# Attention with position bias, two expert layers: score products on 64 rows, the last half tile per head, cheaper relus, weight differences also on GpSimd

## The chip, the cores and the metric

One core of one Trainium2 chip. The metric is the device time of one execution in microseconds, the median of three runs. Five engines work side by side: TensorE (PE, matrix products, with its weight loads PEld), VectorE (DVE), ScalarE (ACT), GpSimd (POOL), and SyncE (SP), which issues the transfers.

## What is computed

Attention over 2 batches, 8 heads, 576 positions, 64 numbers a head, with a bias that a small network makes of the distance of two positions; then a layer of four experts with a gate; then a gated layer.

```python
scores = scale * np.matmul(q, k.transpose(0, 1, 3, 2))
psi_rel = np.log1p(np.abs(rel))
psi_i = np.log1p(np.maximum(pos[:, None].astype(np.float32), 1.0))
x = (psi_rel / psi_i)[..., None]
h = np.maximum(x @ w1 + b1, 0.0)
bias = h @ w2
scores = scores + bias.transpose(2, 0, 1)[None, :, :, :]
scores = scores - np.max(scores, axis=-1, keepdims=True)
attn = np.exp(scores)
attn = attn / (np.sum(attn, axis=-1, keepdims=True) + 1e-09)
return np.matmul(attn, v).astype(np.float32)
...
for e in range(E):
    h = np.maximum(x @ w1[e], 0.0)
    out += p[:, e:e + 1] * (h @ w2[e])
...
return (a * b @ w_out).astype(np.float32)
```

## The kernel before, in words

Everything is written as a list of operations with the engines that may take each, an estimate of its time, a rank and the buffers that it needs; `Plan.run` (L139) walks through the list in estimated time and writes out, engine by engine, the order in which instructions are issued. On the chip each engine follows its own order and waits for semaphores. An operation with `lock` isn't placed on DVE and POOL at the same time as another such.

*Exact products.* PE works on rounded numbers (`fp32r`); to keep precision an operand is split into a rounded part (cast on ACT or DVE) and the rest (a subtraction): `wh`, `wl` for weights (`unit`, L629: cast `whi`, subtraction `wlo`), `qh`, `ql` for queries, `x_hi`, `x_lo` for the layer's input. A product then takes three rounded ones (hi x hi, lo x hi, hi x lo).

*Bias.* `bias_group` (L348) makes 16 rows of the bias at a time, 36 groups: four relus over the table of logarithms, each `max(table * w1 / psi, -b1)` with two operands per partition, three of them on DVE (L357) and one on ACT (L359); four products `pb` on 32-column pieces of the array (L371); `side` and `mirror` write the two arms of the rows (L389, L391; the mirror on POOL is a copy, L396); a transfer stores them in DRAM (`bias_d`, L406). A score tile reads its bias from there (`bt`, L463; three transfers for the last half tile, L465 to L468).

*Attention.* Four pairs of heads `m`, two batches `b`, tiles `t` of 128 queries: t = 0 first for all eight (m, b), then (1, 2) and (3, 4); tile 4 has 64 queries. `step` (L474) takes two heads `s`: scores `ps`, for t = 0 on plain float32 keys and 64-row products, the two key halves on the two row halves of the array (L513); for the others 128-row products (L495): keys lie in 128 partitions, rounded part in the upper 64 and rest in the lower 64, queries are stored twice, so that `qh` and `ql` times these keys are two products for each key half. Then DVE adds the bias and takes the minimum (L498), ACT takes the exponential (L508), PE transposes (`pt`, L524, L541), ACT or DVE copies to `ptb`. Tile 4 puts both heads in one tile of 128 partitions, each with 64 rows. `values` (L554) takes the reciprocals of the sums (L564, L565), spreads them (`rx`, `rp`, `rb`), and makes the products with the values on two column halves (`pv`, L589), and `x_hi`, `x_lo`.

*Fill.* The first expert layer's first pass (`up`, L722; `pz`, L733) needs only tile 0 of all heads. It has rank 2, so it fills what attention leaves of PE; its second pass needs all of attention. The gated layer stands behind.

*Buffers.* Four pairs of weight buffers `w` at first, two of queries `q`, two of values `v`, two raw keys `k2` of 2 x 576.

Of the kernel before, what the change touches and what calls it, by code (L numbers as in the profile page):

```python
# [18 lines left out]
HID = 32  # L19
P = 128  # L20
# [22 lines left out]
           "whi": "ACT DVE", "wlo": "DVE", "xhi": "DVE", "xlo": "POOL DVE", "rb": "ACT DVE", "rx": "ACT DVE", "s64": "POOL DVE",  # L43
# [185 lines left out]
def tile_kernel(ctx, tc, qd, kd, kf, vd, cst, probs, w1r, w2r, war, wbr, wor, out):  # L229
# [57 lines left out]
    place(R["q"], ap_, "q", 2, [P, 2, QW], F32R, pair=True)  # L287
    place(R["k2"], ap_, "k2", 2, [P, 2, S])
    place(R["k"], ap_, "k", 3, [P, 2, S], F32R)
# [11 lines left out]
    place(R["w"], mid, "wm", 2, [P, 1024], F32R, pair=True)  # L301
# [14 lines left out]
    cs_t = hp.tile([P, S + S // 4 + 2 + 32], F32, name="cs")  # L316
    cs, negb = Buf(t=cs_t), hp.tile([P, 1], F32, name="negb")
    corr = {n: hp.tile([P, 1], F32, name=f"corr{n}") for n in sorted(set(RELUS.values()))}
    tab, sc = cs_t[:, 0:S], cs_t[:, S:S + S // 4]
    cw, w2s = cs_t[:, S + S // 4:S + S // 4 + 2], cs_t[:, S + S // 4 + 2:]  # L320
    op({"SP": 440}, lambda e: nc.sync.dma_start(out=cs_t, in_=cst), w=[cs], size=P * 3016)

    def scales(e):
        nc.vector.tensor_scalar(out=sc, in0=sc, scalar1=cw[:, 0:1], scalar2=None, op0=ALU.mult)
        nc.vector.tensor_scalar(out=negb, in0=cw[:, 1:2], scalar1=-1.0, scalar2=None, op0=ALU.mult)
        nc.vector.tensor_scalar(out=w2s, in0=w2s, scalar1=8.0, scalar2=None, op0=ALU.mult)

    op({"DVE": 700}, scales, rw=[cs])
# [19 lines left out]
    def bias_group(u, rank):  # L348
# [24 lines left out]
        op({"PE": n * 1.67 + 250}, mm, r=[*hs, cs], w=[pb], hold=[bst], prio=pri)  # L373


        def ends():
            t, o = base()
            b = bst.t
            if before >= after:
                side = b[:, 0:before + 1], t[:, o:o + 1 + before][:, ::-1]  # L380
                rest = b[:, before + 1:before + after], t[:, o + 1:o + after], b[:, before - after + 1:before][:, ::-1]
            else:
                side = b[:, before:before + after], t[:, o:o + after]
                rest = b[:, 0:before], t[:, o + 1:o + 1 + before][:, ::-1], b[:, before + 1:2 * before + 1][:, ::-1]
            return side, rest

        def put(e, out, src):
            if e == "ACT":
                nc.scalar.activation(out=out, in_=src, func=AF.Identity, bias=corr[acts])  # L389
            else:  # L390
                nc.vector.tensor_scalar(out=out, in0=src, scalar1=corr[acts], scalar2=None, op0=ALU.add)  # L391

        def mirror(e):
            rest = ends()[1]
            if e == "POOL":
                nc.gpsimd.tensor_copy(rest[0], rest[2])  # L396
            else:
                put(e, *rest[:2])
# [3 lines left out]
        op({e: v for e, v in {"POOL": 2 * m + 150, "ACT": m / 1.2 + 280, "DVE": m / 0.96 + 200}.items() if e in ENGINES["mirror"].split()}, mirror, r=[pb, cr], w=[bst], after=[side], prio=pri)  # L402
# [16 lines left out]
    QK, fins = {}, []  # L419
# [9 lines left out]
    def plain(m):  # L429
        k2, q2 = new("k2"), new("q2")  # L430
        op({"SP": 440}, lambda e: nc.sync.dma_start(out=k2.t.rearrange("p b n -> p (b n)"), in_=kf[m]), w=[k2], size=P * 8 * S)
        for b in range(B):
            op({"SP": 440}, lambda e, b=b: nc.sync.dma_start(out=q2.t[:, b].rearrange("p (s w) -> p s w", s=2), in_=qd[m, b][:, :, :P]), w=[q2], size=P * 8 * P)
        return k2, q2

    def keys(m, b):
        k2, k = new("k2"), new("k")
        op({"SP": 440}, lambda e: nc.sync.dma_start(out=k2.t, in_=kd[m, b]), w=[k2], size=P * 8 * S)
        op(t_copy(2 * S, ENGINES["kcast"]), lambda e: copy(e, k.t, k2.t), r=[k2], w=[k], prio=RANK["prep"], lock=True)
        op(t_two(2 * S, ENGINES["ksub"]), lambda e: engine[e].tensor_tensor(out=k.t[D:P], in0=k2.t[D:P], in1=f(k.t[D:P]), op=ALU.subtract), r=[k2], rw=[k], prio=RANK["prep"], lock=True)  # L440
        return k

    def queries(m, b, lo, w):
# [3 lines left out]
        op(t_copy(2 * w, ENGINES["qcast"]), lambda e: copy(e, z(q.t[0]), z(q2.t)), r=[q2], w=[q], prio=RANK["prep"], lock=True)  # L447
# [5 lines left out]
    def bias_tile(m, t):  # L453
# [677 lines left out]
```

## Time and profile before

| | |
|---|---|
| median of 3 runs | 836.31 us (834.63 to 836.48) |
| the profiled execution | 831.73 us, span 830.0 us |
| mean granted clock of PE | 0.997 |
| PE busy | 800.1 us (96%) |
| PE's weight loads | 670.2 us (81%) |
| DVE busy | 615.2 us (74%) |
| ACT busy | 342.7 us (41%) |
| POOL busy | 50.6 us (6%) |
| chain that ended last | PE 83%, DVE 10%, DMA 3%, ACT 3% |

A busy PE is not a PE at its peak: records of its products overlap and last longer than the distance from one start to the next. The time between two starts in a stretch without waits tells what a product costs.

### The profile page before, as it was taken

The page shows a single profiled execution, that of the slowest core. Times are in us where ns is not written, and L with a number is a line of the kernel's source. Part 1 is how long each engine was busy: PE and PEld are TensorE (multiplying, and loading weights), DVE is VectorE, ACT ScalarE, POOL GpSimd, SP SyncE. Part 2 cuts the span into 40 slices and gives each one's busy share as a digit, 9 for nine tenths or more (in the row PEclk, how much of TensorE's full clock was granted, in tenths as well). Part 3 has the DMA queues.
Part 4 walks back from the last instruction along what each step waited for, and adds up shares of the span by engine and source line. Part 5 has one row for each costly group of instructions (what it writes and reads, how often), then busy time and mean ns, then how long its engine had stood idle before and what let it go on. Part 6 is the DMA issues. An engine that isn't in the chain of part 4 may idle for free.

```text
span 830.0 us, 12927 instructions
## 1 busy us (share of the span) xinstructions
PE 800.1 (96%) x4939; PEld 670.2 (81%) x4939; DVE 615.2 (74%) x1245; ACT 342.7 (41%) x694; POOL 50.6 (6%) x63
## 2 busy tenths in 40 slices
PE   7878999999999999999999999999999999999998
PEld 3445677888888788888888988888889999899996
DVE  8898886889977768777988898944656565747545
ACT  7885765566667521122122222213345432323211
POOL 1010000101101000000000000000010100100000
PEclk9999999999999999999999999999999999999999
DMA  6988757677564433664566557610302220201103
GB/s 250 341 276 288 226 178 206 198 234 219 186 202 143 136 87 117 190 217 151 141 190 215 165 152 232 201 74 1 102 1 86 68 77 26 77 31 48 51 1 115
DMA packets 48590, 122.38 MB, mean 147 GB/s; under 512 B 5136, under 2 KB 11536, under 8 KB 48528
## 3 DMA queue, kind: packets, MB, share of 16 engines
q1 hardware_dynamic: 48384, 121.42, 45.9%
q8 instruction: 39, 0.64, 0.3%
q14 instruction: 23, 0.19, 0.1%
q10 hardware_dynamic: 144, 0.13, 0.0%
HBM read 95.69 MB, written 25.84 MB: 146 GB/s over the span
## 4 chain that ended last, share of the span: by engine, by line
PE 83%; DVE 10%; DMA 3%; ACT 3%; issue 1%; POOL 0%; DVEq 0%; SPq 0%; ACTq 0%; POOLq 0%
PE pz L733 31%; PE up L722 22%; PE pw L856 9%; PE pr L856 4%; PE pv L589 4%; PE ps L495 3%; PE pt L524 2%; PE pq L856 2%; DVE pr L498 2%; PE pb L371 2%; DMA bt<-bias_d 1%; DVE wl L633 1%; ACT pr L508 1%; DVE hh L357 1%; DVE k L440 1%
## 5 line engine op out<-in xcount | busy, mean ns | idle before, releaser
L733 PE MATMUL pz<-wh,hh 128*128 128x512 f32 x386 | 154.1, 399 | 0.0
L733 PE MATMUL pz<-wl,hh 128*128 128x512 f32 x386 | 152.2, 394 | 0.0
L733 PE MATMUL pz<-wh,hl 128*128 128x512 f32 x386 | 151.7, 393 | 0.2 <-DVE hl L750 0.2
L722 PE MATMUL up<-x_hi,wh 128*128 128x256 f32 (+2 forms) x384 | 132.9, 346 | 1.2 <-DVE hl L750 1.1
L722 PE MATMUL up<-x_hi,wl 128*128 128x256 f32 (+2 forms) x384 | 129.8, 338 | 0.0
L722 PE MATMUL up<-x_lo,wh 128*128 128x256 f32 (+2 forms) x384 | 129.8, 338 | 0.0
L749 ACT ACTIVATE hh<-up 128x256 fp32r<-128x256 f32 (+2 forms) x96 | 47.0, 491 | 149.1 <-PE up L722 148.9
L236 ACT CAST wh<-wst 128x1024 fp32r<-128x1024 f32 (+1 forms) x62 | 62.4, 1006 | 89.4 <-PE pz L733 79.0
L733 PEld LDWEIGHTS pz<-wl,hh 128*128 128x128 f32 x386 | 72.5, 188 | 17.3
L733 PEld LDWEIGHTS pz<-wh,hl 128*128 128x128 f32 x386 | 72.6, 188 | 15.4 <-DVE hl L750 0.7
L733 PEld LDWEIGHTS pz<-wh,hh 128*128 128x128 f32 x386 | 72.5, 188 | 15.4 <-issue 1.2
L633 DVE TENSOR_TENSOR wl<-wst,wh 128x1024 fp32r<-128x1024 f32 x64 | 78.5, 1229 | 8.2 <-ACT wh L236 6.3
L722 PEld LDWEIGHTS up<-x_hi,wh 128*128 128x128 f32 x384 | 72.3, 188 | 13.2 <-issue 2.8
L722 PEld LDWEIGHTS up<-x_lo,wh 128*128 128x128 f32 x384 | 72.4, 188 | 6.4
L722 PEld LDWEIGHTS up<-x_hi,wl 128*128 128x128 f32 x384 | 72.3, 188 | 5.9
L750 DVE SCALAR_TENSOR_TENSOR hl<-up,hh 128x256 fp32r<-128x256 f32 (+2 forms) x96 | 52.8, 553 | 29.4 <-ACT hh L749 29.0
L498 DVE CUSTOM_DVE_ANT_0 pr<-ps,bt 128x576 f32<-128x576 f32 (+1 forms) x80 | 59.6, 751 | 12.9 <-PE ps L495 9.0
L236 ACT COPY ct<-pw 128x512 f32<-128x512 f32 (+3 forms) x48 | 27.8, 580 | 97.8 <-PE pw L856 97.7
L508 ACT ACTIVATE pr<-pr,sums 128x576 f32<-128x576 f32 x72 | 56.0, 777 | 15.1 <-DVE sums L498 14.6
L357 DVE TENSOR_SCALAR hh<-cs,negb 128x576 f32<-128x576 f32 (+17 forms) x108 | 48.4, 504 | 3.8 <-PE pb L371 3.7
L236 ACT COPY ptb<-pt 128x512 f32<-128x512 f32 (+3 forms) x92 | 38.4, 449 | 26.4 <-PE pt L524 24.8
L524 PE MATMUL pt<-ident,pr 128*128 128x128 f32 x288 | 42.8, 277 | 4.2 <-ACT pr L508 3.5
(157 smaller groups left out, 1408.7 us busy)
## 6 DMA issues: line engine op xcount, KB each, us to landing
wst<-in_w1r SPq DMA_DIRECT2D x32, 512.0 KB, 4.3
wst<-in_w2r SPq DMA_DIRECT2D x32, 512.0 KB, 4.3
bias_d<-bst SPq DMA_DIRECT2D x36, 295.5 KB, 3.9
bt<-bias_d SPq DMA_DIRECT2D x16, 576.0 KB, 5.2
v<-in_vd SPq DMA_DIRECT2D x24, 320.0 KB, 4.6
s<-in_war SPq DMA_DIRECT2D x12, 512.0 KB, 5.1
wz_d<-hl SPq DMA_DIRECT2D x24, 256.0 KB, 2.7
s<-in_wbr SPq DMA_DIRECT2D x12, 512.0 KB, 4.9
```

Of the source, the lines that this page charges most:

```text
L236: (nc.scalar.copy if e == "ACT" else engine[e].tensor_copy)(out, in_)
L357: op({"DVE": n / 1.92 + 190}, lambda e, hh=hh, G=G: nc.vector.tensor_scalar(out=hh.t[:, :n], in0=tab[:, :n], scalar1=sc[:, G:G + 1], scala ...
L498: nc.vector.tensor_tensor_reduce(out=pr.t[r0:r1, c].rearrange("p (a b) -> p a b", a=2), in0=ps.t[r0:r1, :, :HS], in1=bt.t[r0:r1, c].rearra ...
L508: nc.scalar.activation(out=pr.t[:, c], in_=pr.t[:, c], func=AF.Exp, scale=-1.0, bias=sums.t[:, neg:neg + 1], accum_out=sums.t[:, col:col + 1])
L524: nc.tensor.transpose(pt.t[:, kt * P:kt * P + P], pr.t[:, s, k0:k0 + P], ident)
L589: nc.tensor.matmul(pv.t[s * D:(s + 1) * D, :w], V.t[:, s, kt * D:(kt + 1) * D], ptb.t[:, blk, :w], start=(kt == 0), stop=(kt == 4))
L633: op(t_two(1024, ENGINES["wlo"]), lambda e: engine[e].tensor_tensor(out=w.t[1], in0=wst.t, in1=f(w.t[0]), op=ALU.subtract), r=[wst], rw=[w ...
L722: nc.tensor.matmul(u.t[:, :n], a[:, d, ft * P:(ft + 1) * P], x[:, d, lo:lo + n], start=(d == 0 and j == 0), stop=(d == 3 and j == 2))
L733: nc.tensor.matmul(z.t, a[:, ft, tt * P:(tt + 1) * P], bb[:, ft, :], start=(first and ft == 0 and j == 0), stop=(final and ft == 1 and j = ...
L749: relu = op({"ACT": n / 1.2 + 68}, lambda en, ft=ft, u=u: nc.scalar.activation(out=h.t[0][:, ft, :n], in_=u.t[:, :n], func=AF.Relu), r=[u] ...
L750: op({"DVE": n / 0.96 + 68}, lambda en, ft=ft, u=u: nc.vector.scalar_tensor_tensor(out=h.t[1][:, ft, :n], in0=u.t[:, :n], scalar=0.0, in1= ...
L856: nc.tensor.matmul(o_, s[:, k], d[:, k], start=(first and k == 0 and i == 0), stop=(k == 1 and i == 2), skip_group_check=True)
```

## The change

Five edits stand in one version.

1. *Scores.* Keys for t > 0 lie as those for t = 0 did: half the keys in the upper 64 partitions and half in the lower. `k` is a pair (`kh`, `kl`) of 128 x 576, split by a cast and a subtraction of 576 columns instead of 1152. A score takes three terms, (qh, kh), (qh, kl), (ql, kh), each as two 64-row products, one for each key half, on the two row halves of the array.
2. *Last half tile.* Tile 4 handles the two heads one after the other with 64 partitions each: two exponentials, nine transposes of 64 rows, one bias transfer instead of three.
3. *Relus.* The table is multiplied by w1 once (on ACT, ahead of the first relu), and the relu is `max(table, -b1 * psi)` with one operand; the division by psi and the correction move into `side`, which multiplies and adds. The mirror is a copy on each engine that may take it.
4. *Weight differences.* `wlo` may go to POOL or DVE, and not to DVE alone.
5. *Buffers.* Raw keys and queries come per (m, b); at the start there is one pair of weight buffers and one of query buffers less, and two raw queries and two values more; when eight of these have been given out, the extra ones return to weights and queries.

```diff
-           "whi": "ACT DVE", "wlo": "DVE", "xhi": "DVE", "xlo": "POOL DVE", "rb": "ACT DVE", "rx": "ACT DVE", "s64": "POOL DVE",
+           "whi": "ACT DVE", "wlo": "POOL DVE", "xhi": "DVE", "xlo": "POOL DVE", "rb": "ACT DVE", "rx": "ACT DVE", "s64": "POOL DVE",
...
+    op({"ACT": S / 1.2 + 200}, lambda e: nc.scalar.activation(out=tab, in_=tab, func=AF.Copy, scale=cw[:, 0:1]), r=[cs], w=[lg], prio=-1)
...
-                op({"DVE": n / 1.92 + 190}, lambda e, hh=hh, G=G: nc.vector.tensor_scalar(out=hh.t[:, :n], in0=tab[:, :n], scalar1=sc[:, G:G + 1], scalar2=negb, op0=ALU.mult, op1=ALU.max), r=[cs], w=[hh], prio=pri, lock=True)
+                op({"DVE": n / 1.92 + 130}, lambda e, hh=hh, G=G: nc.vector.tensor_scalar(out=hh.t[:, :n], in0=tab[:, :n], scalar1=neg_[:, G:G + 1], scalar2=None, op0=ALU.max), r=[cs], w=[hh], prio=pri, lock=True)
...
-                nc.vector.tensor_scalar(out=out, in0=src, scalar1=corr[acts], scalar2=None, op0=ALU.add)
+                nc.vector.tensor_scalar(out=out, in0=src, scalar1=rinv[:, u:u + 1], scalar2=corr[acts], op0=ALU.mult, op1=ALU.add)
...
-        k2, k = new("k2"), new("k")
-        op({"SP": 440}, lambda e: nc.sync.dma_start(out=k2.t, in_=kd[m, b]), w=[k2], size=P * 8 * S)
-        op(t_copy(2 * S, ENGINES["kcast"]), lambda e: copy(e, k.t, k2.t), r=[k2], w=[k], prio=RANK["prep"], lock=True)
-        op(t_two(2 * S, ENGINES["ksub"]), lambda e: engine[e].tensor_tensor(out=k.t[D:P], in0=k2.t[D:P], in1=f(k.t[D:P]), op=ALU.subtract), r=[k2], rw=[k], prio=RANK["prep"], lock=True)
+        k2, k = raw_keys(m, b), new("k")
+        op(t_copy(S, ENGINES["kcast"]), lambda e: copy(e, k.t[0], k2.t), r=[k2], w=[k], prio=RANK["prep"], lock=True, after=guests[-2:])
+        op(t_two(S, ENGINES["ksub"]), lambda e: engine[e].tensor_tensor(out=k.t[1], in0=k2.t, in1=f(k.t[0]), op=ALU.subtract), r=[k2], rw=[k], prio=RANK["prep"], lock=True)
...
-                for kk, qz in enumerate(Q.t):
-                    lhs = qz.rearrange("p s w -> p (s w)")[:, at:at + P]
-                    for n, (half, o, k0, w) in enumerate(runs):
-                        nc.tensor.matmul(ps.t[:, half, o:o + w], lhs, K.t[:, s, k0:k0 + w], start=(kk == 0 and n < 2), stop=(kk == 1 and n in (0, len(runs) - 1)))
+                terms = [(Q.t.rearrange("p s w -> p (s w)"), K.t)] if t == 0 else [(Q.t[i].rearrange("p s w -> p (s w)"), K.t[j]) for i, j in ((0, 0), (0, 1), (1, 0))]
+                for i, (q, kt) in enumerate(terms):
+                    for half in range(2):
+                        r = slice(half * D, half * D + D)
+                        nc.tensor.matmul(ps.t[:n, half, :HS], q[r, at:at + n], kt[r, s * HS:s * HS + HS], start=(i == 0), stop=(i == len(terms) - 1))
...
-            op({"PE": 640}, qk_plain, r=[Q, K, bt], w=[ps], hold=[pr, sums]) if t == 0 else op({"PE": 560 if len(runs) == 2 else 700}, qk, r=[Q, K, bt], w=[ps], hold=[pr, sums])
+            o = op({"PE": 680 if t == 0 else 470}, qk, r=[Q, K, bt], w=[ps], hold=[pr, sums])
...
-                k0 = kt * P + (D if t < 4 and s else 0)
-                nc.tensor.transpose(pt.t[:, kt * P:kt * P + P], pr.t[:, s, k0:k0 + P], ident)
+                k0 = kt * P + D * s
+                nc.tensor.transpose(pt.t[:, kt * n:kt * n + n], pr.t[:n, s, k0:k0 + P], ident[:n, :n])
```

Where the orders differ, on PE behind the bias groups of the first stage (`k_100`, `k_109` are raw keys, `q_102`, `q_111` raw queries). Before:

```order
L371 MATMUL pb<-hh,cs 32x416 x4
L371 MATMUL pb<-hh,cs 32x400 x4
L513 MATMUL ps<-k_100,q_102 128x288 x8
L524 MATMUL pt<-ident,pr 128x128 x4
L513 MATMUL ps<-k_109,q_111 128x288 x4
```

Now:

```order
L379 MATMUL pb<-hh,cs 32x416 x4
L379 MATMUL pb<-hh,cs 32x400 x4
L379 MATMUL pb<-hh,cs 32x384 x4
L379 MATMUL pb<-hh,cs 32x368 x4
L379 MATMUL pb<-hh,cs 32x352 x4
L379 MATMUL pb<-hh,cs 32x336 x4
L490 MATMUL ps<-k_100,q_102 128x288 x4
L490 MATMUL ps<-k_104,q_106 128x288 x4
L490 MATMUL ps<-k_112,q_114 128x288 x4
```

Four more bias groups stand ahead of the first score, and the scores follow without a transpose between them.

On PE among the fill, scores of tiles above 0. Before:

```order
L733 MATMUL pz<-wl,hh 128x512
L495 MATMUL ps<-k,qh 128x288 x2
L495 MATMUL ps<-k,ql 128x288 x2
L722 MATMUL up<-x_hi,wh 128x256
L722 MATMUL up<-x_lo,wh 128x256
```

Now, where a tile of 128 and a tile of 64 queries meet:

```order
L697 MATMUL pz<-wl,hh 128x512
L490 MATMUL ps<-kh,qh 128x288 x2
L490 MATMUL ps<-kl,qh 128x288 x2
L490 MATMUL ps<-kh,ql 128x288 x2
L514 MATMUL pt<-ident,pr 128x64 x4
L697 MATMUL pz<-wh,hh 128x512
```

Each score group is now three pairs of 64-row products with 128-row products on either side.

On POOL, in the middle of attention. Before:

```order
L396 COPY bst<-bst 128x95
L396 COPY bst<-bst 128x15
L448 TENSOR_TENSOR ql<-q_1452,qh 128x512
L448 TENSOR_TENSOR ql<-q_1516,qh 128x512
L598 TENSOR_TENSOR x_lo<-xf,x_hi 128x192
L598 TENSOR_TENSOR x_lo<-xf,x_hi 128x256
```

Now:

```order
L236 COPY bst<-bst 128x47
L236 COPY bst<-bst 128x15
L597 TENSOR_TENSOR wl<-wst,wh 128x1024 x4
L564 TENSOR_TENSOR x_lo<-xf,x_hi 128x192
L597 TENSOR_TENSOR wl<-wst,wh 128x1024 x3
L564 TENSOR_TENSOR x_lo<-xf,x_hi 128x256
```

45 of the 64 weight differences stand on POOL, 26 of them up to the end of attention; 19 are left on DVE.

## Rows read from the trace of the kernel before

**Rows 1.** The page, DVE's busy tenths in 40 equal slices of the span
```profile
DVE  8898886889977768777988898944656565747545
```

**Rows 2.** Busy time by stretch; columns are named in the first line
```profile
core 0: us, PE busy (x) PEld busy (x) DVE busy (x) ACT busy (x) POOL busy (x), PEclk, DMA share, GB/s
0.00:77.44 77.44, 60.34 (x538) 34.00 (x538) 66.43 (x181) 58.34 (x123) 9.25 (x21) 0.98 0.84 292
77.44:295.19 217.75, 210.99 (x1593) 172.48 (x1592) 176.56 (x392) 138.41 (x306) 20.97 (x23) 1.00 0.62 193
```

**Rows 3.** Timeline of DVE at the start: start us, us, engine, line, operation
```profile
4.03 0.29 DVE L324 TENSOR_SCALAR cs<-cs 128x144 f32<-128x144 f32 x1 [4.03 <-DMA cs<-in_cst]
```

**Rows 4.** Groups by line and form, whole span: xcount | busy us, mean ns
```profile
L633 DVE TENSOR_TENSOR wl<-wst,wh 128x1024 fp32r<-128x1024 f32 x64 | 78.5, 1229 | 8.2 <-ACT wh L236 6.3 <-DMA bt<-bias_d 1.3 <-DVE x_lo L598 0.2
...
L498 DVE CUSTOM_DVE_ANT_0 pr<-ps,bt 128x576 f32<-128x576 f32 x64 | 47.6, 751 | 9.4 <-PE ps L495 6.0 <-DMA bt<-bias_d 2.9 <-PE ps L513 0.4
...
L440 DVE TENSOR_TENSOR k<-k,k 64x1152 fp32r<-64x1152 f32 x8 | 11.4, 1428 | 0.2
...
L357 DVE TENSOR_SCALAR hh<-cs,negb 128x576 f32<-128x576 f32 x6 | 3.2, 574 | 0.0
...
L236 DVE CAST k<-k 128x1152 fp32r<-128x1152 f32 x4 | 3.0, 754 | 0.0
...
L448 DVE TENSOR_TENSOR ql<-q,qh 128x512 fp32r<-128x512 f32 x4 | 2.7, 681 | 0.0
```

**Rows 5.** PE's score products: one line's durations (min/median/max), and timelines
```profile
L513 PE MATMUL ps<-k,q x64: 402/403/507, 23.1 to 54.6; 64*128 64x288 f32 x64
...
26.90 1.19 PE L513 MATMUL ps<-k,q 64*128 64x288 f32 x6 [2.57 <-DVE sums L498]
...
265.75 0.42 PE L495 MATMUL ps<-k,qh 128*128 128x288 f32 x2
266.02 0.42 PE L495 MATMUL ps<-k,ql 128*128 128x288 f32 x2
...
288.64 0.54 PE L495 MATMUL ps<-k,qh 128*128 128x288 f32 x3
...
289.37 0.65 PE L524 MATMUL pt<-ident,pr 128*128 128x128 f32 x4
289.87 0.27 PE L541 MATMUL pt<-ident,pr 128*128 128x128 f32 x1
```

**Rows 6.** Timeline of PE, a bias group between fill products
```profile
81.27 0.28 PE L722 MATMUL up<-x_hi,wl 128*128 128x256 f32 x1
81.48 0.85 PE L371 MATMUL pb<-hh,cs 128*32 128x384 f32 x8
82.27 0.38 PE L722 MATMUL up<-x_hi,wh 128*128 128x256 f32 x1
82.49 0.28 PE L722 MATMUL up<-x_lo,wh 128*128 128x256 f32 x1
82.61 0.29 PE L722 MATMUL up<-x_hi,wl 128*128 128x256 f32 x1
```

**Rows 7.** Chain of waits, bias groups: start us, us, what
```profile
79.89 0.76 PE pb L371 x8
...
106.93 0.97 PE pb L371 x8
```

**Rows 8.** Waits of PE's weight loads, 77.44 to 295.19: us in total, times, longest
```profile
PEld ps L495 <- DVE sums L498: 5.3, 9, 1.3
PEld pt L524 <- ACT pr L508: 3.2, 4, 1.6
...
PEld up L722 <- DVE hl L750: 2.2, 4, 0.7
```

**Rows 9.** Timelines of POOL and DVE in attention
```profile
211.25 1.31 POOL L448 TENSOR_TENSOR ql<-q,qh 128x512 fp32r<-128x512 f32 x1 [3.13 <-DVE qh L236]
...
251.00 2.07 POOL L448 TENSOR_TENSOR ql<-q,qh 128x512 fp32r<-128x512 f32 x1 [9.68 <-DVE qh L236]
...
251.82 1.27 DVE L564 TENSOR_SCALAR sums<-sums 128x3 f32<-128x3 f32 x1
```

More of the change, by code (lines that the diff above doesn't have):

```diff
@@ L300, in tile_kernel @@
     place(R["w"], right, "w", 2, [P, 1024], F32R, pair=True)
-    place(R["w"], mid, "wm", 2, [P, 1024], F32R, pair=True)
+    place(R["w"], mid, "wm", 1, [P, 1024], F32R, pair=True)
+    for z in "hl":
+        R["v"].add(lambda name, z=z: mid.tile([P, 1024], F32, tag=f"wx0{z}", name=name, bufs=1)[:, :10 * D].rearrange("p (s d) -> p s d", s=2), mark="early")
     place(R["wst"], right, "wst", 2, [P, 1024])
@@ L504, in ttr @@
                 )
-            def ex(e, c=c, neg=neg):
-                col = 2 * k + c
-                nc.scalar.activation(out=pr.t[:, c], in_=pr.t[:, c], func=AF.Exp, scale=-1.0, bias=sums.t[:, neg:neg + 1], accum_out=sums.t[:, col:col + 1])
-            def qk_plain(e, s=s, ps=ps):
-                for half in range(2):
-                    r = slice(half * D, half * D + D)
-                    nc.tensor.matmul(ps.t[:, half, :HS], Q.t[r, b, s * P:s * P + P], K.t[r, b, s * HS:s * HS + HS], start=True, stop=True)
@@ L556, in values @@
         rp, pv = new("tv", "rp"), new("tv", "pv")
[L557 to L558 removed]
+        parts = [(P, 0, sum(t < 4 for t in ts))]
+        if 4 in ts:
+            parts.append((D, parts[0][2], 1))
         def recip(e):
[L563 to L571 removed]
@@ L573, in spread_copy @@
-        def spread_copy(e):
-            if 4 in ts:
-                for s in range(2):
-                    x = slice(s * D, (s + 1) * D)
-                    copy(e, rb.t[x, n:w], rp.t[x, n + s * D:n + (s + 1) * D])
-            copy(e, rb.t[:, :n], rp.t[:, :n])
-        o = op({"DVE": 300}, recip, rw=[sums], prio=RANK["fin"])
-        op(t_copy(n, ENGINES["rx"]), lambda e: copy(e, rx.t[:, :full], sums.t[:, 0:2 * full].rearrange("p (t s) -> p t s", s=2).unsqueeze(3).to_broadcast([P, full, 2, D])), r=[sums], w=[rx], prio=RANK["fin"], after=[o])
+            for n, k, c in parts:
+                x = sums.t[:n, 2 * k:2 * k + 2 * c]
+                nc.vector.tensor_scalar(out=x, in0=x, scalar1=1e-9, scalar2=None, op0=ALU.add)
+                nc.vector.reciprocal(out=x, in_=x)
@@ new lines, in widen @@
+        def widen(e):
+            for n, k, c in parts:
+                copy(e, rx.t[:n, k:k + c], sums.t[:n, 2 * k:2 * k + 2 * c].rearrange("p (t s) -> p t s", s=2).unsqueeze(3).to_broadcast([n, c, 2, D]))
+        def spread(e):
+            for n, k, c in parts:
+                for t in range(k, k + c):
+                    nc.tensor.transpose(rp.t[:, t * P:t * P + n], rx.t[:n, t].rearrange("p s d -> p (s d)"), ident[:n, :n])
+        o = op({"DVE": 300 * len(parts)}, recip, rw=[sums], prio=RANK["fin"])
```

171 lines of the change are left out of this document (77 added, 94 removed).

## The prediction

> **What bounds the kernel now.** I read the page's forty slices first. They show DVE at 80 to 90% for the first third and at about half from there on [rows 1]. Then I cut the span where the program itself changes: at 77.44 us the first product of the first expert layer starts (I call these products the fill, since they take every gap that attention leaves on PE), and at 295.19 us the last attention product is out and the second pass begins [rows 2]. The reader is to see three stages. Before 77.44 PE is busy for 60 of 77 us and DVE for 66: no fill exists yet, and what decides is how soon DVE (relus, score reductions, key splits) lets the eight first-tile groups end. From 77.44 to 295.19 PE is busy for 211 of 217.75 us, DVE for 177. Behind that come 535 us in which PE never rests; no instruction of the change stands there but the weight differences that go to GpSimd.
>
> So a gain can come from three places only: an earlier 77.44, less PE work between the two marks, and fewer waits between them. I sum these three.
>
> **First stage: DVE.** Counted in the two built orders, DVE issues 187 instructions ahead of its first fill instruction before, 188 now. One-operand relus: a two-operand one of 576 columns takes 574 ns [rows 4], the one-operand multiply at 4.03 takes 0.29 us for 144 columns [rows 3]. At 0.52 ns a column (an estimate that leaves the 754 ns of the 1152-column cast [rows 4] a plausible fixed part of 155) the fixed parts are 274 and 215 ns, so each relu loses about 60 ns: 72 x 0.06 = -4.3 us. Three more relus stand ahead of the fill, near 0.4 each (+1.2). Keys: before three casts of 1152 columns and three subtractions of 64x1152, 3 x (0.75 + 1.43) = 6.5 us [rows 4]; now two casts and three subtractions of 576 columns, about 2 x 0.4 + 3 x 0.74 = 3.0: -3.5. Two weight differences fewer, -2.5; two score reductions fewer, 2 x 0.75 = -1.5 [rows 4]. One cast and two 512-column copies more, about 0.7 each (the 512-column row of [rows 4]): +2.1. The table is now multiplied by w1 on ACT before the first relu: +0.5. The sum is -8.0. DVE's few waits in this stage stay, so I take **-7 us** (bounds -3, if loads or ACT end it instead, and -9).
>
> **Second stage: PE's work.** Scores: a regular group was four 288-column products, two of them in 0.27 us; a 64-row product streams the same columns, and two halves run side by side: six records of 0.40 us of the first tiles took 1.19 us in all, where one after another they would take 2.4 [rows 5]. So three pairs cost three such products and save 0.134 us; 56 x 0.134 = 7.5. The eight groups of the second head's last half tile took six products, 0.73 us; three pairs take 0.40 [rows 5]: 8 x 0.33 = 2.6. Together -10.1. The last half tile is now transposed per head, nine transposes for six; four take 0.50 [rows 5], so 24 x 0.12 = +2.9. Two score groups that stood ahead of the fill now stand behind it: +1.
>
> Then the cut of the array, which the change alters most often. A bias group (32-column pieces) between fill products: from the product at 81.27 to the second one behind the group, at 82.49, 1.22 us pass [rows 6]. Two of the 0.12 us products are 0.24. The group itself streams: the chain's bias groups of 368 and of 496 columns lie 0.97 - 0.76 = 0.21 us apart [rows 7], so its 384 columns take 0.63. The 0.35 us left over are two changes of cut: the first piece starts 0.21 us after its neighbour instead of 0.12, the first product behind it loads its weights uncovered. I take **0.18 us a change**. From below 0.09 (the late start alone, the load hidden by a wait); from above 0.20, since a 64-row piece has a 128-column load, and the first pair after a change took 507 ns for 402 [rows 5]. Counted in the built orders between the first fill product and the last attention product, PE changes its cut 58 times before; now 155 times, or 177 if the 64-row transposes count. That is +97 to +119, x 0.18 = +17.5 to +21.4. PE's work: -10.1 + 2.9 + 1 + 19 = **+13 us** (from +2 to +18).
>
> The Trainium skill, TensorEngine Tiling (Array Packing), section Theoretical Speedup, promises up to twofold for a contraction of at most 64 rows. By it alone, with no price on a change of cut, PE's work would fall by 6 us and the kernel would end near 817 us. Its section Key Properties says that a change of mode drains the array, and names no price; the 0.35 us of the rows agree with that.
>
> **Second stage: waits.** PE's weight loads waited 5.3 us for DVE's score sums, 2.2 for the fill's low halves and 3.2 for ACT's exponentials [rows 8], some 12 us with the small ones. 29 of the 35 weight differences of this stage leave DVE (6 remain, 26 stand on GpSimd): 29 x 1.23 = 36 us [rows 4], and DVE falls from 81% to some 65%. In the built order the last fill product has 15 rows of attention behind it instead of 43, so the bare tail shrinks. I take **-6** (bounds -10 and +3).
>
> What costs nothing: ACT's eight more exponentials, since ACT is busy for 138 of 218 us [rows 2]; the halved key loads and one bias load in place of three on SP's queue; one pair of weight buffers and one of query buffers fewer at the start, as these places come back when the eight first-tile groups have their values, about when the fill begins. If that cover goes, the first weight pieces are late by a cast.
>
> **Third stage.** The 19 differences on GpSimd take at most 2.6 us each, twice the 1.31 us of 512 columns undisturbed [rows 9]; PE never rests here and uses a unit of weights for several microseconds: 0.
>
> **Sum.** -7 + 13 - 6 = 0. The profiled execution took 831.73 us beside its span of 830.0, 4.6 below the median of 836.31; on the median I forecast **836 us**, no change.
>
> **Rivals.**
> *Cheap changes of cut (faster).* If most changes fall where PE waits anyway, or cost the 0.09 us of the late start alone, PE's work grows by +2 to +4: -7 + 3 - 4 = -8, **828 us**. At no price at all the sum is -7 - 6 - 6 = -19, 817 us, 0.03 of this rival's chance. For it: scores wait for DVE in 9 places [rows 8], and such a wait swallows an entry. Against it: in the built order most score groups now stand between fill products, where nothing waits.
> *GpSimd stands in DVE's way (slower).* At 251.82 a three-column add on DVE took 1.27 us, until GpSimd's subtraction ended, and that subtraction took 2.07 us instead of 1.31 [rows 9]. The Trainium skill, GPSIMD Engine Reference, section 1. Specifications, says that GpSimd's SBUF interfaces are shared with VectorE, for DVE instructions with two SBUF inputs or in a two-port mode; these rows agree. Now 26 subtractions of up to 2.6 us, 68 us in all, lie over attention, and the reciprocals, the widening copies and the splits are of that kind. If half of the 26 hold up such an instruction by 1 us, and it is the one that PE's next row needs, the waits grow by 13 instead of shrinking by 6, less what DVE's freed third absorbs: +8 on the sum, **844 us**. It decides once more than about six PE rows are late by it. Against it: reductions and low halves, which read PSUM, ran beside GpSimd at their usual time, and DVE has room.
> *The halves don't run side by side.* Then 64 groups pay 0.4 us more each, +25, **861 us**. The six records above speak against it.
>
> **Chances.** The forecast 0.48, with a range of its own of 832 to 841; cheap changes 0.28; GpSimd 0.18; halves 0.02; something not seen 0.04. A measurement of this kernel tells 0.2% (1.7 us) from no change. Faster: 0.28 and a fifth of the forecast's case, 0.38. Same: half of that case, 0.24. Slower: 0.18, 0.06 and the rest of it, 0.38. The range reaches to the centres of both near rivals: 826 to 845.
>
> **What would show it.** Right: the first fill product at 69 to 72 us; relus of 576 columns near 0.43 us apart; a score group between fill products costs about 0.75 us up to the second product behind it; the last attention product ends at 292 to 298 us, and 535 us follow. Wrong: a first fill product later than 75 us, score groups of 0.6 us or less, DVE adds of over 1 us in tens, or a third stage that differs by more than 2 us.

## The result and the profile after

The changed kernel took **846.62 us** (844.82 to 847.84, four runs) beside 835.47 us for the kernel before: a ratio of 1.0131, with a 95% interval of 1.0110 to 1.0151. It is 11 us slower; 836 had been forecast, with a range up to 845. The profiled execution had a span of 844.0 us; the kernel before happened to be profiled in one of its faster executions (830.0 us), so the stages below lie 14.0 us apart in all and the medians 11.

The three stages, found anew at the first fill product and at the last attention product, answer to [rows 2]. Busy time by stretch of the changed kernel, and behind it four slices of 1 us from its second stage:

```profile
core 0: us, PE busy (x) PEld busy (x) DVE busy (x) ACT busy (x) POOL busy (x), PEclk, DMA share, GB/s
0.00:74.97 74.97, 57.85 (x528) 31.91 (x528) 61.29 (x184) 55.33 (x115) 10.46 (x18) 0.95 0.84 284
74.97:306.47 231.50, 223.27 (x1741) 167.30 (x1737) 159.56 (x389) 142.90 (x314) 80.66 (x43) 0.98 0.56 172
306.47:844.00 537.53, 528.97 (x2812) 463.51 (x2811) 373.52 (x656) 147.90 (x268) 55.94 (x34) 1.00 0.36 110
...
205.00:206.00 1.00, 0.00 (x0) 0.00 (x0) 1.00 (x1) 0.00 (x0) 1.00 (x1) 1.00 0.13 41
206.00:207.00 1.00, 0.20 (x2) 0.23 (x3) 1.00 (x3) 0.00 (x0) 0.24 (x1) 0.88 0.00 0
207.00:208.00 1.00, 1.00 (x7) 0.88 (x7) 0.67 (x3) 0.50 (x2) 0.00 (x0) 0.50 0.00 0
...
213.00:214.00 1.00, 1.00 (x8) 0.33 (x6) 0.00 (x0) 0.00 (x0) 0.00 (x0) 0.71 0.12 45
```

Against [rows 2] the first stage is 2.5 us shorter, the second 13.7 longer, the third (534.8 us before) 2.7 longer. In the second, TensorE is busy for 12.3 us more, and its granted clock is 0.98 where it was 1.00. The small slices show one of two places where that comes from: at 205 us VectorE and GpSimd are busy for the whole microsecond and TensorE does nothing; from 207 on TensorE is busy all the time, but at a granted clock of 0.50, the lower of its two levels (1.2 GHz), until about 213.6. The other place is a stretch from 172.6 to 176.0 us.

What happened ahead of that stands in the timeline of the same kernel (start us, us, engine, line, operation, and in brackets the idle time before and what ended it):

```profile
164.73 4.72 POOL L597 TENSOR_TENSOR wl<-wst,wh 128x1024 fp32r<-128x1024 f32 x2 [4.90 <-ACT wh L236]
165.60 1.52 DVE L534 TENSOR_SCALAR sums<-sums 128x2 f32<-128x2 f32 x1
167.16 0.17 DVE L535 RECIPROCAL sums<-sums 128x2 f32<-128x2 f32 x1
167.24 2.23 DVE L534 TENSOR_SCALAR sums<-sums 64x2 f32<-64x2 f32 x1
...
170.92 0.40 PE L490 MATMUL ps<-kh,qh 64*128 64x288 f32 x2 [1.50 <-DVE sums L493]
...
201.57 4.67 POOL L597 TENSOR_TENSOR wl<-wst,wh 128x1024 fp32r<-128x1024 f32 x2 [3.59 <-ACT wh L236]
201.98 4.34 DVE L236 COPY rx<-sums 128x128 f32<-128x128 f32 x2
...
206.25 0.41 DVE L561 TENSOR_TENSOR xf<-pv,rb 128x256 f32<-128x256 f32 x1
...
206.80 0.66 PE L514 MATMUL pt<-ident,pr 64*128 64x64 f32 x4 [3.26 <-DVE xf L561]
207.39 0.58 PE L686 MATMUL up<-x_hi,wh 128*128 128x256 f32 x1
207.77 0.41 PE L686 MATMUL up<-x_lo,wh 128*128 128x256 f32 x1
```

Two weight differences stand on GpSimd in a row from 201.57 to 206.24. VectorE's two widening copies, 0.2 to 0.3 us apiece when nothing is in the way, take 4.34 us in all and end with the second difference. VectorE's multiplication `xf` is queued behind them, and the transposes on TensorE wait 3.26 us for the PSUM place that `xf` frees. At 165 us it is the same with two adds of two columns, 1.52 and 2.23 us where 0.14 to 0.16 is usual; TensorE then waits 1.50 us for a reduction queued behind them. The reciprocal between the two adds, which is SBUF-only as well, took its usual 0.17 us beside the second difference, and so did the three other reciprocals that met one. Between the two stage marks nine VectorE instructions take over 1 us more than others of their form; before there was one, the add of [rows 9]. By this trace 31 of the 45 differences start on GpSimd before the last attention product ends, 29 of them in the second stage; the built order had 26 up to the end of attention.

### The profile page after: what moved, and what is told of

The parts are those of the page before. It is cut to its first block, busy times and chain, and to the rows that moved or that the text cites. A ratio compares the mean times of both kernels' runs of the same rounds, so it can differ in the third digit from the quotient of the medians.

```text
span 844.0 us, 13209 instructions
## 1 busy us (share of the span) xinstructions
PE 810.1 (96%) x5075; PEld 662.7 (79%) x5075; DVE 594.4 (70%) x1228; ACT 346.1 (41%) x696; POOL 147.1 (17%) x95
## 4 chain that ended last, share of the span: by engine, by line
PE 85%; DVE 8%; DMA 3%; ACT 2%; issue 1%; POOL 1%; SPq 0%; DVEq 0%; POOLq 0%; ACTq 0%
PE pz L697 30%; PE up L686 23%; PE pw L820 9%; PE ps L490 5%; PE pr L820 4%; PE pt L514 4%; PE pv L555 4%; PE pq L820 2%; PE pb L379 2%; DVE pr L493 1%; DMA bias_d<-bst 1%; DVE sums L534 1%; DMA s<-in_wor 1%; PE pz L900 1%; PE rp L544 1%
## 5 line engine op out<-in xcount | busy, mean ns | idle before, releaser
L597 POOL TENSOR_TENSOR wl<-wst,wh 128x1024 fp32r<-128x1024 f32 x45 | 108.4, 2410 | 266.1 <-ACT wh L236 148.9
L686 PEld LDWEIGHTS up<-x_hi,wh 128*128 128x128 f32 x384 | 72.6, 189 | 12.6 <-issue 3.8
L503 ACT ACTIVATE pr<-pr,sums 128x576 f32<-128x576 f32 (+1 forms) x80 | 62.1, 776 | 21.3 <-DVE sums L493 20.4
L514 PE MATMUL pt<-ident,pr 128*128 128x128 f32 (+1 forms) x320 | 47.9, 279 | 6.8 <-DVE xf L561 4.1
L236 ACT COPY ptb<-pt 128x512 f32<-128x512 f32 (+3 forms) x77 | 35.6, 477 | 37.8 <-PE pt L514 32.6
L514 PEld LDWEIGHTS pt<-ident,pr 128*128 128x128 f32 (+1 forms) x320 | 34.9, 145 | 18.4 <-issue 9.9
```

What stands on the lines that cost most here:

```text
L236: (nc.scalar.copy if e == "ACT" else engine[e].tensor_copy)(out, in_)
L503: nc.scalar.activation(out=pr.t[:n, s], in_=pr.t[:n, s], func=AF.Exp, scale=-1.0, bias=sums.t[:n, neg:neg + 1], accum_out=sums.t[:n, col:c ...
L514: nc.tensor.transpose(pt.t[:, kt * n:kt * n + n], pr.t[:n, s, k0:k0 + P], ident[:n, :n])
L597: op(t_two(1024, ENGINES["wlo"]), lambda e: engine[e].tensor_tensor(out=w.t[1], in0=wst.t, in1=f(w.t[0]), op=ALU.subtract), r=[wst], rw=[w ...
L686: nc.tensor.matmul(u.t[:, :n], a[:, d, ft * P:(ft + 1) * P], x[:, d, lo:lo + n], start=(d == 0 and j == 0), stop=(d == 3 and j == 2))
```

## The experiments

**1 to 4: GpSimd's differences against the array's cut, each undone alone and together.** E1 is one word in the table of engines:

```diff
-           "whi": "ACT DVE", "wlo": "POOL DVE", "xhi": "DVE", "xlo": "POOL DVE", "rb": "ACT DVE", "rx": "ACT DVE", "s64": "POOL DVE",
+           "whi": "ACT DVE", "wlo": "DVE", "xhi": "DVE", "xlo": "POOL DVE", "rb": "ACT DVE", "rx": "ACT DVE", "s64": "POOL DVE",
```

> The changed kernel with its 45 weight differences back on VectorE, all else kept. Theory GpSimd (the differences on GpSimd hold up reciprocals and widening copies, PE waits for them and its clock falls): 8 to 12 us come back, 834 to 839 us; no VectorE add or copy of over 1 us between the first fill product and the last attention product (9 in the changed kernel), and no second-stage slice at half clock. Theory cut (the 100 more changes of the array's cut are the loss, GpSimd is harmless): 844 to 850 us, since VectorE takes back 36 us of work there.

Measured: 833.73 us, ratio to the kernel before 0.9984 (0.9970 to 0.9999). Its stages:

```profile
0.00:72.70 72.70, 56.99 (x521) 32.06 (x521) 59.66 (x179) 53.77 (x112) 6.51 (x17) 0.98 0.83 282
72.70:296.44 223.74, 220.06 (x1749) 164.44 (x1745) 175.42 (x414) 144.84 (x324) 13.56 (x16) 1.00 0.57 180
296.44:832.20 535.76, 529.22 (x2811) 463.54 (x2811) 371.91 (x673) 145.87 (x266) 20.03 (x19) 1.00 0.35 111
```

All of the loss is gone, and the second stage runs at full clock, though VectorE has 16 us more to do in it. One add is still held for over 1 us, as in the kernel before; GpSimd has a query difference there.

E2 is the opposite word in the kernel before.

```diff
-           "whi": "ACT DVE", "wlo": "DVE", "xhi": "DVE", "xlo": "POOL DVE", "rb": "ACT DVE", "rx": "ACT DVE", "s64": "POOL DVE",
+           "whi": "ACT DVE", "wlo": "POOL DVE", "xhi": "DVE", "xlo": "POOL DVE", "rb": "ACT DVE", "rx": "ACT DVE", "s64": "POOL DVE",
```

> The kernel before with nothing but leave for GpSimd to take weight differences. Theory GpSimd: 840 to 847 us, with several VectorE adds or copies of over 1 us (1 in the kernel before) and one or more stretches at half clock after a wait. Theory cut: 831 to 836 us, as VectorE is relieved of some 36 us and the cuts stay as they were.

Measured: 841.82 us, 1.0080 (1.0057 to 1.0103): slower, though nothing else of the change is there. 37 differences went to GpSimd, seven VectorE instructions up to the last attention product took over 1 us more than others of their form, and the granted clock was 0.50 in three stretches (one in the kernel before). Only one of the three, at 170.7 us, lies in the second stage; the two in the first stage follow no held instruction of that length. The second stage is 226.1 us long, 8.3 more than before.

E3 leaves the differences on GpSimd and takes back the 64-row products, with the keys stacked as the kernel before has them; its main lines:

```diff
-                        nc.tensor.matmul(ps.t[:n, half, :HS], q[r, at:at + n], kt[r, s * HS:s * HS + HS], start=(i == 0), stop=(i == len(terms) - 1))
...
+                            nc.tensor.matmul(ps.t[:n, half, :HS], q[:, at:at + n], K.t[s][:, half * HS:half * HS + HS], start=(i == 0), stop=(i == 1))
```

> The changed kernel with the scores behind the first tiles as 128-row products again (keys stacked high over low, four 288-column products a group); the differences stay on GpSimd, the last half tile stays per head. Theory GpSimd: still 841 to 848 us, since the held-up copies stay. Theory cut: some 100 changes of cut go, at 0.10 to 0.18 us each 10 to 18 us, for 8 us more of streaming: 836 to 842 us.

Measured: 847.56 us, 1.0145 (1.0118 to 1.0172). E4 has both edits, that of E1 and that of E3.

> Both undone: 128-row scores and the weight differences on VectorE; the one-operand relus, the per-head last half tile and the key loads of the change stay. Theory GpSimd: 832 to 837 us, near the run that undoes GpSimd alone, less what the cuts cost net of streaming (2 to 8 us). Theory cut: 834 to 840 us, no better than the 128-row run alone.

Measured: 833.66 us, 0.9995 (0.9976 to 1.0015). So the four corners are 846.6 and 847.6 us with the differences on GpSimd, 833.7 and 833.7 without: GpSimd costs 13 to 14 us whichever form the scores have, and the form of the scores costs and brings nothing that these runs can tell. Each of the four has an order of instructions planned anew, so these differences hold the effect of the order too.

**5: the same program with GpSimd's instruction cut in four.** This one leaves the order of the instructions on every engine as the change has it; only each of the 45 differences is now four instructions in a row.

```diff
+        def lo(e):
+            step = 256 if e == "POOL" else 1024
+            for i in range(0, 1024, step):
+                engine[e].tensor_tensor(out=w.t[1][:, i:i + step], in0=wst.t[:, i:i + step], in1=f(w.t[0][:, i:i + step]), op=ALU.subtract)
...
-        op(t_two(1024, ENGINES["wlo"]), lambda e: engine[e].tensor_tensor(out=w.t[1], in0=wst.t, in1=f(w.t[0]), op=ALU.subtract), r=[wst], rw=[w], prio=RANK["split"], lock=True)
+        op(t_two(1024, ENGINES["wlo"]), lambda e: lo(e), r=[wst], rw=[w], prio=RANK["split"], lock=True)
```

> The changed kernel with each weight difference on GpSimd issued as four instructions of 256 columns in a row (one of 1024 columns took 2.41 us; one of 256 columns takes about 0.75). Theory hold-to-the-end (an SBUF-only VectorE instruction waits for the end of the GpSimd instruction that runs): holds shrink to 0.75 us at most, no VectorE add or copy of over 1 us is left, 836 to 841 us. Rival, whole-run (VectorE waits until GpSimd is through with its row of instructions, or the planner's changed order is what costs): still 844 to 850 us with holds near 2 us.

Measured: **832.84 us**, 0.9984 (0.9964 to 1.0003), below what either theory expected. Its stages:

```profile
0.00:73.44 73.44, 56.03 (x528) 31.29 (x528) 60.90 (x184) 55.34 (x115) 11.19 (x24) 1.00 0.84 289
73.44:293.26 219.82, 218.19 (x1741) 164.44 (x1737) 150.47 (x389) 142.81 (x314) 92.91 (x130) 1.00 0.59 181
293.26:831.90 538.64, 530.32 (x2811) 464.68 (x2811) 367.30 (x656) 147.84 (x268) 70.33 (x76) 1.00 0.35 109
```

The differences by group, of this kernel and then of the changed one (count, busy us, mean ns):

```profile
L599 POOL TENSOR_TENSOR wl<-wst,wh 128x256 fp32r<-128x256 f32 x180 | 137.2, 794 | 247.1 <-ACT wh L236 128.8 <-DVE wh L236 74.3 <-PE up L692 19.5
```

```profile
L597 POOL TENSOR_TENSOR wl<-wst,wh 128x1024 fp32r<-128x1024 f32 x45 | 108.4, 2410 | 266.1 <-ACT wh L236 148.9 <-DVE wh L236 82.4 <-DMA wst<-wz_d 10.1
```

And the widening copies on VectorE (durations in ns: min/median/max), again of this kernel and then of the changed one:

```profile
L236 DVE COPY rx<-sums x19: 197/227/767, 34.0 to 288.9; 128x128 f32<-128x128 f32 x11, 128x256 f32<-128x256 f32 x4, 64x128 f32<-64x128 f32 x4
```

```profile
L236 DVE COPY rx<-sums x19: 198/227/2377, 34.6 to 302.0; 128x128 f32<-128x128 f32 x11, 128x256 f32<-128x256 f32 x4, 64x128 f32<-64x128 f32 x4
```

GpSimd is busier by 29 us with the differences, and the kernel is 13.8 us faster by the medians (1.5% by the ratios). The longest copy falls from 2377 to 767 ns, about one piece: a VectorE instruction of this kind is held to the end of the GpSimd instruction that it meets, and no longer. In the second stage no VectorE instruction takes over 1 us more than others of its form. With the same order on both sides the second stage can be split: 231.50 - 219.82 = 11.7 us, of which TensorE's idle time is (231.50 - 223.27) - (219.82 - 218.19) = 6.6 and its busy time 5.1. The slices of 1 us at a lowered clock (around 172 to 176 and 206 to 214) fall short of the full clock by 5.1 us in all. So the waits cost 6.6 us and the clock after them 5.1.

The Trainium skill, SBUF — State Buffer, section Who interferes with whom, says that VectorE and GpSimd share one pair of ports by an exclusive lock, for VectorE instructions in a two-port mode or with two SBUF inputs, and that whoever issues first keeps it for a whole instruction while the other one blocks fully. The 2377 and 767 ns agree with the lock; whether the adds and copies ran in such a mode no row shows.

**6: GpSimd for the second expert pass alone.** Most of these differences stand behind attention.

```diff
-            WU[p, e, q, 0] = unit(w1r[e, q])
+            WU[p, e, q, 0] = unit(w1r[e, q], "wlo" if p else "wlo2")
...
-            WU[p, e, q, 1] = unit(w2r[e, q])
+            WU[p, e, q, 1] = unit(w2r[e, q], "wlo" if p else "wlo2")
```

> The changed kernel with the weight differences of the first expert pass on VectorE; only those of the second pass, most of them behind attention, may go to GpSimd. Theory GpSimd-in-attention: the second stage comes back to about 224 us as with all differences on VectorE, the third stage stays 1 to 3 us longer than before: 834 to 838 us. Rival (the third stage suffers as much per difference as attention): 839 to 843 us.

Measured: 834.25 us, 0.9999 (0.9982 to 1.0015), with the stages at 72.05, 224.58 and 536.57 us. It is attention that suffers: 13 VectorE instructions of the third stage are held for over 1 us here, as many as in the changed kernel (one in the kernel before), and yet the time is that of E1. The third stage pays about 1 us against the 535.8 of E1, within what two profiles differ by.

**7: the price of a change of cut, by itself.** In E1, one product in six of the second pass's second layer goes over 64 rows alone (the other half of that contraction is left out, so a part of the sum is missing from the output).

```diff
-                    nc.tensor.matmul(z.t, a[:, ft, tt * P:(tt + 1) * P], bb[:, ft, :], start=(first and ft == 0 and j == 0), stop=(final and ft == 1 and j == 2))
+                    r = slice(0, D if cut and ft == 1 and j == 0 else P)
+                    nc.tensor.matmul(z.t, a[r, ft, tt * P:(tt + 1) * P], bb[r, ft, :], start=(first and ft == 0 and j == 0), stop=(final and ft == 1 and j == 2))
```

> The changed kernel with the differences on VectorE and, in the second pass's second expert layer, one of the six products of every step taken over the upper 64 rows alone (the other 64 rows of that product are left out, so that part of the sum is missing from the output): the product streams its 512 columns as ever, but stands between 128-row products, so the array's cut changes twice. The steps lie where TensorE never rests, 112 of them. Theory 0.18 a change (an excursion costs 0.34 to 0.37 us): 833.7 + 38 to 41 = 872 to 875 us. Rival 0.09 to 0.10 a change, the late start alone: 833.7 + 20 to 22 = 854 to 856 us. Rival free: 834 us.

Measured: 876.32 us, 1.0509 (1.0470 to 1.0547). Its third stage, and the timeline of TensorE around one such product:

```profile
295.57:874.50 578.93, 572.49 (x2811) 454.21 (x2811) 373.72 (x673) 145.74 (x266) 20.02 (x19) 1.00 0.34 103
```

```profile
502.31 0.39 PE L698 MATMUL pz<-wh,hl 128*128 128x512 f32 x1
502.54 0.40 PE L698 MATMUL pz<-wl,hh 128*128 128x512 f32 x1
502.87 0.50 PE L698 MATMUL pz<-wh,hh 64*128 64x512 f32 x1
503.30 0.50 PE L698 MATMUL pz<-wh,hl 128*128 128x512 f32 x1
503.63 0.40 PE L698 MATMUL pz<-wl,hh 128*128 128x512 f32 x1
503.87 0.40 PE L698 MATMUL pz<-wh,hh 128*128 128x512 f32 x1
```

(578.93 - 535.76) / 112 = 0.385 us an excursion (to 64 rows and back), 0.19 a change; the time lies just above the 872 to 875 us expected. The starts show where it falls: 0.23 us is the usual distance, the 64-row product starts 0.10 late, its successor 0.20 late, and the one behind that 0.10 late.

**8 and 9: the bias part.** E8 puts it alone into the kernel before, E9 takes it out of E1. The main lines of it, as E8 has them (of the relu's line the call alone):

```diff
-nc.vector.tensor_scalar(out=hh.t[:, :n], in0=tab[:, :n], scalar1=sc[:, G:G + 1], scalar2=negb, op0=ALU.mult, op1=ALU.max)
+nc.vector.tensor_scalar(out=hh.t[:, :n], in0=tab[:, :n], scalar1=neg_[:, G:G + 1], scalar2=None, op0=ALU.max)
...
-                nc.scalar.activation(out=out, in_=src, func=AF.Identity, bias=corr[acts])
+                nc.scalar.activation(out=out, in_=src, func=AF.Identity, scale=rinv[:, u:u + 1], bias=corr[acts])
```

> The kernel before with the bias part of the change alone: table scaled once on ScalarE, one-operand relus, the reciprocal distance in the evacuation, plain mirror copies. Theory VectorE bounds the first stage: 72 relus lose 60 ns each, the first fill product comes 3 to 5 us earlier (73 to 75 us) and the time falls to 830 to 833 us. Rival (the groups' evacuations on ScalarE bound it): first fill product at 76 to 78 us, 834 to 837 us.

Measured: 849.16 us, 1.0177 (1.0148 to 1.0207), which neither theory has room for. Its first stage:

```profile
0.00:104.18 104.18, 78.25 (x594) 40.86 (x594) 74.38 (x206) 68.93 (x141) 10.32 (x19) 0.87 0.72 242
```

> The changed kernel with the differences on VectorE and the bias part taken back: two-operand relus, the table unscaled, the evacuation without the reciprocal distance. Theory VectorE bounds the first stage: the first fill product comes 3 to 5 us later than the 72.7 us with one-operand relus, 75.5 to 78 us, and the time rises to 836 to 839 us. Rival (ScalarE's evacuations bound it, or the relus' gain is used up elsewhere): first fill product at 71 to 74 us, 832 to 835 us.

Measured: 837.51 us, 1.0038 (1.0021 to 1.0054), where E1 has 0.9984: with the bias part E1 is some 0.5%, or 4 us, faster. But the mark was missed: the first fill product came at 61.68 us, with 15 bias groups ahead of it in the built order (22 in E1), and attention ended at 299.46 (296.44 in E1). In E8 29 groups stand ahead of it (22 before), TensorE stops often and its granted clock is 0.87 for 104 us. The planner's estimates for the new relus shift the order, but that E8's 15 us in the wrong direction come from this shift is argued, not shown. A run with the order of the kernel before and the new relus was not made, so the relus' price stays open in both kernels.

**10: pieces in the first pass, VectorE in the second.** The edit of E5, and the engine of a unit's difference chosen as in E6 with the two names the other way round (`wlo2` is VectorE alone).

```diff
-            WU[p, e, q, 1] = unit(w2r[e, q])
+            WU[p, e, q, 1] = unit(w2r[e, q], "wlo2" if p else "wlo")
```

> The changed kernel with the differences of the first expert pass in four pieces on GpSimd and those of the second pass on VectorE. The second stage should stay near the 220 us of the run in pieces, the third fall from its 538.7 to some 535.5 us: 829 to 831.5 us, faster than the kernel before. Rival (the third stage's 4 us were one late low half by chance of the planned order): 832 to 834 us.

Measured: 833.05 us, 0.9979 (0.9966 to 0.9992), inside the rival's range. The third stage fell to 535.1 us as expected, but the first two together took 296.1 where E5 took 293.3. Beside E1 it is the only version whose interval lies below 1, by a hair; it can't be told from E1 and E5.

**11: telling the planner.** Whole differences on GpSimd; reciprocals and widening copies are marked so that the plan doesn't put them beside GpSimd's.

```diff
-        o = op({"DVE": 300 * len(parts)}, recip, rw=[sums], prio=RANK["fin"])
-        op({e: v + 68 * (len(parts) - 1) for e, v in t_copy(2 * w, ENGINES["rx"]).items()}, widen, r=[sums], w=[rx], prio=RANK["fin"], after=[o])
+        o = op({"DVE": 300 * len(parts)}, recip, rw=[sums], prio=RANK["fin"], lock=True)
+        op({e: v + 68 * (len(parts) - 1) for e, v in t_copy(2 * w, ENGINES["rx"]).items()}, widen, r=[sums], w=[rx], prio=RANK["fin"], after=[o], lock=True)
```

> The changed kernel with whole differences on GpSimd, the reciprocals and widening copies now marked for the planner as work that must not stand beside GpSimd's (as the splits are). Theory hold: most holds of over 1 us go, and with them most of the loss, 834 to 840 us; a few stay, as the plan's clock runs apart from the chip's. Rival (the plan's clock is too far off to help): 842 to 848 us.

Measured: 839.73 us, 1.0064 (1.0045 to 1.0083): about half. In the second stage no add or widening copy is held for over 1 us any more, but four instructions that had been marked all along are. One of them, 0.75 us otherwise, in its timeline:

```profile
159.42 2.81 POOL L597 TENSOR_TENSOR wl<-wst,wh 128x1024 fp32r<-128x1024 f32 x1 [4.40 <-DVE rb L236]
...
159.91 2.94 DVE L447 TENSOR_TENSOR kl<-k,kh 128x576 fp32r<-128x576 f32 x1
```

The plan keeps the two apart by its own clock, and on the chip they meet.

**12: the last half tile of both heads together again,** on E4, with the functions for it as the kernel before has them; its main lines:

```diff
-        for s in range(2):
+        for s in range(2 if t < 4 else 1):
...
-                exps.append(op({"ACT": 770}, ex, after=[red], w=[sums], hold=[pr]))
+            if t < 4 or s == 1:
+                exps.append(op({"ACT": 770}, ex, after=[red] if t < 4 else [red, half0], w=[sums], hold=[pr]))
```

> The run with 128-row scores and the differences on VectorE, with the last half tile of both heads in one tile again. Of the change only the bias part and the key loads per batch element are left. Theory: the last half tile per head neither gave nor took (scores -2.6, transposes +2.9 us): 832 to 836 us, as the 833.7 with it. Rival (eight more exponentials and reductions, or more changes of cut, cost something): 829 to 831 us.

Measured: 839.51 us, 1.0057 (1.0037 to 1.0076), against 0.9995 with the half tile per head. In these two planned orders a half tile per head is worth some 5 us, which no theory had. In the second stage TensorE is busy for less with the joined tile (214.65 against 218.48 us) but idle for 13.5 us against 7.0. The joined tile has one exponential that waits for both heads' reductions; how much of the idle time that makes, and how much the order, was not separated. This version is also 0.6% slower than the kernel before, though little of the change is left in it. Edit 5, the buffers, was in no run undone or put in by itself.

## Why the prediction was wrong

**The step that failed is the second stage's waits,** "I take -6", where +6.6 was measured: 1.5 us more idle time of TensorE and 5.1 us of half clock. The step let 29 differences leave VectorE and counted only what that frees. On GpSimd each is an instruction of 2.4 us, and short VectorE instructions of the attention chain were held behind it. With the same order and short instructions (E5) the idle time of TensorE is 1.6 us against 6.8 before: -5.1, nearly what the step said. With the long ones it is 8.2, and the half clock comes on top.

The rival "GpSimd stands in DVE's way" named the place and the mechanism and gave 844 us; its chance, 0.18, was too low, and the range stopped 1 us above it. That its 844 came so near is partly luck: its terms, -7 + 13 + 13, make +19, and the 11 us that VectorE's freed time was to absorb stand in no row. Of the instructions it named, adds, widening copies and splits were held, the reciprocals not. What was held against it is true and did not help: instructions that read PSUM did run undisturbed, for example the 576-column reductions at 753 ns beside a difference and without one, and VectorE had room (69% busy in that stage), but room on average doesn't help an add that the next transpose waits for. [Rows 9] had shown a hold of this kind at half the length. No step had the clock: a wait of 3.26 us was followed by 6.8 us at 1.2 GHz.

The misses of the four terms are +4.5 us (first stage), +12.6 (waits), -5.8 (TensorE's work) and +2.7 (third stage), together the 14.0 us between the two profiled executions. Of the prediction's own signs, the last attention product ended at 306.5 us (292 to 298 said) and the third stage differs by more than 2 us; adds of over 1 us came singly, not in tens.

**First stage,** -7 forecast, -2.5 measured. The relus lost what was said: the 576-column one of [rows 4] took 574 ns, and in the changed kernel, by group (count, busy us, mean ns):

```profile
L365 DVE TENSOR_SCALAR hh<-cs 128x576 f32<-128x576 f32 x6 | 2.8, 516 | 0.1
```

With the differences on VectorE the stage gains 4.7 us (E1), in pieces 4.0, so 1.5 to 2.3 us of the miss came with the whole differences on GpSimd; the stage's granted clock is 0.95 with them, 0.98 in E1 and 1.00 in E5. What is still short of 7 fits ScalarE's evacuations, but no run takes these away. This is the changed kernel's longest wait of TensorE ahead of the first fill product (us in all, times, longest), and the kernel before has none of its kind:

```profile
PE pb L379 <- ACT bst L397: 5.3, 8, 1.3
```

The bound of -3 "if loads or ACT end it" named this place.

**TensorE's work,** +13 forecast. E5 shows +7.2 us of busy time (218.19 - 210.99), the changed kernel +12.3, the difference being the 5.1 us of half clock. The price of a change, 0.18 us, agrees with E7's 0.19, measured for one kind of change in the third stage; the count agrees too: 179 against 74 in the two traces, +105 where +97 to +119 was said. A score group between fill products costs 0.82 us up to the second product behind it (0.75 said), from 84.77 to 85.59 in the changed kernel:

```profile
84.56 0.28 PE L686 MATMUL up<-x_hi,wl 128*128 128x256 f32 x1
84.77 0.40 PE L490 MATMUL ps<-kh,qh 64*128 64x288 f32 x2
85.01 0.29 PE L490 MATMUL ps<-kl,qh 64*128 64x288 f32 x2
85.14 0.29 PE L490 MATMUL ps<-kh,ql 64*128 64x288 f32 x2
85.36 0.39 PE L686 MATMUL up<-x_hi,wh 128*128 128x256 f32 x1
85.59 0.28 PE L686 MATMUL up<-x_lo,wh 128*128 128x256 f32 x1
```

The 6 us that the sum has too much were not traced.

The Trainium skill, TensorEngine Tiling (Array Packing), section Theoretical Speedup, allows up to twice the speed for such products. The corners of E1 to E4 show none of it in the time. That the cuts around short groups take it back is argued from the price of E7, not shown by a run of its own.

**Third stage,** 0 forecast, +2.7 measured. With the differences on VectorE it is 535.8 (E1), +1. With them on GpSimd it is 537.5 here, but 534.6 in E2 and 536.0 in E3, so the price depends on the order. TensorE waited 2.1 us for low halves here, 0.2 before; the longer wait is in the last line of this timeline of the changed kernel:

```profile
387.89 2.40 POOL L597 TENSOR_TENSOR wl<-wst,wh 128x1024 fp32r<-128x1024 f32 x1 [5.13 <-DMA wst<-in_w1r]
388.19 2.38 DVE L618 TENSOR_SCALAR t<-t 128x512 uint32<-128x512 uint32 x1
...
392.89 1.76 POOL L634 TENSOR_TENSOR s<-s,hl 128x512 f32<-128x512 f32 x1 [2.60 <-ACT hh L713]
393.41 1.53 DVE L614 TENSOR_SCALAR t<-s 128x512 uint32<-128x512 uint32 x1
...
395.31 1.48 DVE L714 SCALAR_TENSOR_TENSOR hl<-up,hh 128x384 fp32r<-128x384 f32 x3
395.92 0.50 PE L697 MATMUL pz<-wh,hl 128*128 128x512 f32 x1 [1.79 <-DVE hl L714]
```

Two VectorE instructions ahead of the low half are held, 2.38 and 1.53 us where 0.42 is usual, the first by a weight difference, the second by another subtraction on GpSimd. The step looked at TensorE's use of the weights alone, and not at what else stands in VectorE's queue.

**What was right, and what was luck:** without the holds the change is worth -1.3 us (E5) to -1.7 us (E1) by the medians, so no change was the right forecast for everything but the 45 differences. That it came out so is partly luck. By the stages of E5 the four terms are -4.0, +7.2, -5.1 and +3.8 us where -7, +13, -6 and 0 were said: three are off by 3 to 6 us, and the errors cancel.

## What to carry to other kernels

Before work is moved to GpSimd, look at how long one of its instructions is, not at how busy the engines are: the adds, widening copies, relus and splits of VectorE that met one here waited for its end, up to 2.4 us. Cut it into pieces that are as short as the instructions beside it. Where TensorE is the bound, price a wait by what follows too: after one of 3.3 us the array ran at half its clock for 6.8 us, after one of 1.5 us for 3.4. And where a planner makes a new order for each version, as it did in E8, which was 15 us slower with cheaper relus, a cause is safest shown by a run that keeps the order, as E5 does.

## What was not expected of the hardware

- Between two GpSimd instructions in a row one held VectorE instruction got through, and the next one was held again: the two copies at 201.98 took 4.34 us, beside 4.67 us of GpSimd.
- Not every SBUF-only VectorE instruction is held: the four reciprocals of the changed kernel that met a difference took 0.16 to 0.18 us, as ever.
- A change of cut isn't paid on entry alone: 0.10 us on the 64-row product, 0.20 on its successor, 0.10 on the one behind.
- The half-clock stretch outlasted the wait before it: TensorE was busy again from 206.8 us, and the granted clock was at 0.50 until after 213.
